# Narrow memory sums, a narrower masked copy, two more DMA transposes and a new instruction order in a planned attention and feed-forward kernel

## The chip, the cores and the metric

The kernel runs on one core of one Trainium2 chip. The metric is the device time of one execution in microseconds (us). Each engine of the core (PE for matrix products, DVE, ACT and POOL for elementwise work, SP for issuing transfers) takes its own list of instructions in the order in which the program holds them, and waits on semaphores for the others. The profile is that of one execution.

## The reference, cut to what matters

Two layers, each an attention block and a gated feed-forward block, run over 2048 tokens of width 512. Attention works on four segments of 512 tokens with 32 heads of width 16. Inside a segment it is causal softmax; across segments there is a memory: a 16x16 matrix M and a vector z for each head, to which every segment adds.

```python
for s in range(N):
    logits = jnp.einsum('bhqd,bhkd->bhqk', qs, ks) * scale + mask
    p = _softmax(logits, axis=-1)
    a_dot = jnp.einsum('bhqk,bhkd->bhqd', p, vs)
    pq = phi(qs)
    num = jnp.einsum('bhld,bhde->bhle', pq, M)
    den = jnp.einsum('bhld,bhd->bhl', pq, z)[..., None] + 1e-06
    a_mem = num / den
    o = g * a_mem + (1.0 - g) * a_dot
    outs.append(o)
    pk = phi(ks)
    M = M + jnp.einsum('bhld,bhle->bhde', pk, vs)
    z = z + jnp.einsum('bhld->bhd', pk)
...
x = x + _A_ref(_layernorm(x, axis=-1), A_wq, A_wk, A_wv, A_wo, A_beta)
x = x + _B_ref(_layernorm(x, axis=-1), B_w_gate, B_w_up, B_w_down)
```

The feed-forward block is `_gelu(x @ w_gate) * (x @ w_up) @ w_down` with an inner width of 1792. This pair of lines stands twice.

## The kernel before

All weights and all of x stay in on-chip memory. There are eight units of work k = 0..7 (two layers by four segments), each with an attention part (`Att`, L610 on) and a feed-forward part (`Ffn`, L1018 on). Everything is made of 128x128 by 128x512 products on PE.

**The planner.** The program is straight-line code whose order is made while it is built. `order` (L286) keeps a model clock for each engine (`Engine`, `Clocks`), a list of work items for PE (`Item`: due time, readiness, products, what follows) and jobs posted to the other engines. Its main loop (L1425 on) takes, at each step, two rounds of attention scores if they are due, or the ready item with the least due time, and writes its instructions out. The engines' lists come out in that order. The numbers in `POLICY` (L69) weigh these choices: due times, slacks, and margins. Three matter here. `lag` (L1446): items are first looked for that have been ready for `lag` us, then those that are ready now. `margin` (L567, L706): the transfers that make `xnT` and `vz` are taken to be there 1.4 us plus `margin` after their issue has ended; those that make `phik` and the turned memory result `amT`, 1.4 us after it. `FILL` (L65): how many tiny products stand ahead of each transposition on PE, to cover a wait. Where no item is ready and scores are still to come, a fill product of `warm` is written (L1464).

**Attention of a unit.** The rows are normalised (`Norm`), turned to the layout that PE wants (`xnT`), and multiplied by wq, wk and wv. `xnT` is made on PE by `turn_item` (four transposing products for each 128 rows, L586, then a copy out of PSUM) for the units that `by_pe` names (attention k = 1 and 2, since `pe_turns` is 2; feed-forward 0, 1 and 7), else by a transposing transfer that SP issues (`turn_later`, L431). Scores are made in 36 rounds for a unit on four row tiles (`score_round`, L938), exponentiated by ACT (L1398), masked by POOL or DVE (L1345, L1350, L1355), and summed against v by `flush_item` (L954) in four column tiles. Odd heads and the round that even and odd heads share use masked copies of k (`masked_copies`, L411 on): for even heads a copy 128 columns wide for each 128 rows, of which 64 are then overwritten by the odd heads' copy.

**Memory of a unit.** For segments 0 to 2 `phi` makes pk on ACT, POOL and DVE, SP turns it by a transfer (`phik`), and `upd_item` (L852) sums pk times v: 16 products of 128x128 by 128x128 into a PSUM bank of 4x128 columns, of which only the 16x16 blocks on the diagonal are wanted. DVE masks them with `bd` to `mblk` (L878) and keeps the running sum `macc` (L893, L895).

**PE's modes.** A product is either whole (128x128 weights, L476) or split into four 32-column tiles that run side by side (L471); `product` picks the split form when PE is in column tiles already or when a flush is near.

Of the kernel before, what the change touches and what calls it, by code (L numbers as in the profile page):

```python
# [12 lines left out]
ALU = mybir.AluOpType  # L13
# [18 lines left out]
VALUES = TPS * VW + 16  # L32
SCALE = DH ** -0.5
# [11 lines left out]
PAIRED = [(ki, P * ki, C, C * ki) for ki in range(TPS)]  # L45


def round_of(t):

    b, i = divmod(t, ROUNDS)  # L50
    if i == SHARED:
        return b, (0, 1), PAIRED, None
    par = int(i > SHARED)
    return b, (par,), FULL[i - par * (SHARED + 1)], DIAG[i - par * (SHARED + 1)]


BY_PE = {("xnTf", 0), ("xnTf", 1), ("xnTf", NK - 1)}
BANKS = 8
# [3 lines left out]
URGENT, SOON, NORMAL = -4.0, -1.5, 0.0  # L62
XN_BUFS = 4
BUFS = 6
FILL = 2  # L65
# [4 lines left out]
    flush_wait=31.348, piece_slack=5.108, kb_slack=25.115, mem_slack=-15.103, margin=2.314, qk_due=0.572,  # L70
    e_q=-1.218, e_k=1.714, exp_slack=-25.107, e_slack=9.023, phi_slack=17.383, gelu_slack=6.274,
    act_evict=8.464, first_evict=0.965, gate_step=0.061, up_due=-0.553, up_step=0.062, down_due=2.078,
# [3 lines left out]
    col_gap=3.33, hold=8, early=4.123, starve=0.308, near=-1.576, cap=4, soon=9.685, columns=0)  # L76
# [15 lines left out]
class Engine:  # L92
# [24 lines left out]
    def serve(self, now):  # L117
# [9 lines left out]
        job = min((j for j in jobs if j[0] + self.LATENCY <= start + 0.03), key=lambda j: j[0] + j[1] + (  # L127
# [123 lines left out]
class Item:  # L251


    def __init__(self, due, ready, ops, done, kind, ps, after="start"):
        self.after = after
        self.due = due if callable(due) else lambda: due
        self.ready, self.ops, self.done, self.kind, self.ps = ready, ops, done, kind, ps
        self.posted = 0.0
# [27 lines left out]
def order(pol, nc, cst, seg, wrk, psp, A_x, A_wq, A_wk, A_wv, A_wo, A_beta, B_x, B_w_gate, B_w_up, B_w_down, out):  # L286
# [88 lines left out]

    tmp_e2 = cst.tile([P, H], F32, name="tmp_e2")
    cden = cst.tile([P, H], BF16, name="cden")
    macc = cst.tile([P, 4, P], F32, name="macc")
# [32 lines left out]
    def masked_copies(ready, slack, kx, kf, told):  # L411
# [4 lines left out]
        def vector(which, eng):  # L416
            return lambda: eng.tensor_scalar(out=kx[:, :, C * which:C * which + P], in0=kf, scalar1=masks[:, which:which + 1],  # L417
                                             scalar2=None, op0=ALU.mult)
# [6 lines left out]
        ck.dve.post(ready, slack, (Port(0.35), vector(0, nc.vector), None),  # L425
                    (Port(0.35), vector(1, nc.vector), told), taken=taken)
        ck.pool.post(ready, slack + pol.kb_pool, (Port(1.57, True), vector(0, nc.gpsimd), None),
# [50 lines left out]
    def soon(name, n=KT, part=1.0):  # L478

        t = ck.pe - 0.1 - ck.back  # L480
# [20 lines left out]
    class Norm:  # L501
        def __init__(self, key, tt0, tag, slack, free):
            self.key, self.tt0, self.tag, self.slack, self.free = key, tt0, tag, slack, free
            self.mv, self.n, self.left = None, 0, TPS
# [3 lines left out]

        def stats(self, j, ready):
            def emit():  # L510
                if self.mv is None:
                    self.mv = self.small("mv", 2)
# [3 lines left out]
            def told(t):  # L516
                self.n += 1
                if self.n == TPS:
                    self.scales(t)

            ck.dve.post(ready, self.slack, (0.66, emit, None),
                        (0.17, lambda: nc.vector.bn_aggr(out=self.mv[:, j, :], in_=self.st6[:]), told))  # L522

        def scales(self, ready):
            def first():
                self.ve = wrk.tile([P, TPS, 1], F32, tag="lnve", name="ve")
                nc.gpsimd.tensor_scalar(out=self.ve[:], in0=self.mv[:, :, 1:2], scalar1=EPS_LN, scalar2=None,
                                        op0=ALU.add)

            def second():  # L530
                self.rs = self.small("rs", 1)
                nc.gpsimd.tensor_tensor(out=self.rs[:], in0=self.ve[:], in1=mhalf[:], op=ALU.pow)  # L532

            ck.pool.post(ready, URGENT, (0.25, first, None),
                         (1.05, second, lambda t: ck.when(self.free, lambda: self.start(max(t, ck.pe)))))

        def start(self, ready):
            self.xnT = seg.tile([P, KT, L], BF16, tag=self.tag, bufs=1, name="xnT")
            for j in range(TPS):
                xn_slots.take(lambda n, j=j: bufs.take(lambda i: self.row(j, n, i, max(ready, ck.pe))))  # L540

        def normed(self, j, i, eng=nc.vector):
            xn = buffer(i, "xn")
            eng.tensor_scalar(out=xn[:], in0=x_sb[:, self.tt0 + j, :], scalar1=self.mv[:, j, 0:1],  # L544
# [3 lines left out]
        def row(self, j, n, i, ready):  # L548
# [13 lines left out]
            def told(t):  # L562
                if self.by_pe():
                    items.append(self.turn_item(j, xn, t, landed))
                else:
                    turn_later(t, self.slack, lambda: self.xnT[:, :, j * P:(j + 1) * P], lambda: xn()[:], landed,
                           pol.margin)  # L567

            on_dve_or_pool(ready, self.slack, pol.xn_pool if self.key[0] == "xnTa" else None, Port(0.405),
# [5 lines left out]
        def turn_item(self, j, xn, t, landed):  # L575
# [4 lines left out]
            def turned():  # L580
# [8 lines left out]
                        lambda: evict(ps, lambda: self.xnT[:, :, j * P:(j + 1) * P], turned, landed, URGENT),  # L589
# [937 lines left out]
```

## Time and profile before

| | |
|---|---|
| time, median of 3 runs | 544.17 us (544.15 to 544.77) |
| span of the profiled execution, first to last instruction | 542.6 us |
| PE busy | 527.1 us, 97% |
| DVE busy | 443.1 us, 82% |
| ACT busy | 434.4 us, 80% |
| POOL busy | 305.9 us, 56% |

The profile lists no time for the profiled execution other than its span. The median of the runs is 1.6 us longer than that span; this is taken as what lies around the first and the last instruction. In the rows below, a group reads: line, engine, operation, output and inputs by name, shape, count, then busy time and the mean duration of one instruction. A row of the timeline begins with its start and its length in us. Products on PE overlap, so a duration is not a cost: the cost of one is the distance from its start to the next one's start.

### The profile page before, as it was taken

The page shows a single profiled execution, that of the slowest core. Times are in us where ns is not written, and L with a number is a line of the kernel's source. Part 1 is how long each engine was busy: PE and PEld are TensorE (multiplying, and loading weights), DVE is VectorE, ACT ScalarE, POOL GpSimd, SP SyncE. Part 2 cuts the span into 40 slices and gives each one's busy share as a digit, 9 for nine tenths or more (in the row PEclk, how much of TensorE's full clock was granted, in tenths as well). Part 3 has the DMA queues.
Part 4 walks back from the last instruction along what each step waited for, and adds up shares of the span by engine and source line. Part 5 has one row for each costly group of instructions (what it writes and reads, how often), then busy time and mean ns, then how long its engine had stood idle before and what let it go on. Part 6 is the DMA issues. An engine that isn't in the chain of part 4 may idle for free.

```text
span 542.6 us, 21272 instructions
## 1 busy us (share of the span) xinstructions
PE 527.1 (97%) x9271; PEld 274.9 (51%) x9332; DVE 443.1 (82%) x816; ACT 434.4 (80%) x540; POOL 305.9 (56%) x359
## 2 busy tenths in 40 slices
PE   8999989999999999999999999999999999999997
PEld 4454455454545444544544555545465456555444
DVE  7898999799988999879987998889586797786342
ACT  6999989988998989989799798996879977930320
POOL 4897786369846788349993468716753265300000
PEclk9999999999999999999999999999999999999999
DMA  8306510610331123310312250211420105100001
GB/s 268 98 13 192 117 23 17 171 35 20 51 50 24 24 40 61 41 38 9 41 32 50 33 71 4 40 33 23 79 52 3 22 13 89 24 3 25 16 0 40
DMA packets 64784, 26.94 MB, mean 50 GB/s; under 512 B 49074, under 2 KB 64690, under 8 KB 64690
## 3 DMA queue, kind: packets, MB, share of 16 engines
q1 hardware_dynamic: 64400, 25.31, 22.7%
q8 instruction: 73, 1.20, 0.9%
q10 hardware_dynamic: 290, 0.26, 0.2%
q14 instruction: 21, 0.17, 0.1%
HBM read 9.70 MB, written 2.10 MB: 22 GB/s over the span
## 4 chain that ended last, share of the span: by engine, by line
PE 83%; DVE 12%; issue 2%; DMA 2%; ACT 0%; POOL 0%; SPq 0%; DVEq 0%; ACTq 0%
PE ps L476 44%; PE ps L471 25%; PE ps L938 7%; PE ps L954 6%; DVE st L514 2%; DVE x_sb L1027 1%; DVE xn L544 1%; DVE byq L971 1%; DMA phik<-e 1%; DVE phiq L745 1%; DVE mv L522 1%; DMA x_sb<-in_A_x_dram 0%; DMA amT<-am 0%; DVE e L745 0%; ACT pt L1398 0%
## 5 line engine op out<-in xcount | busy, mean ns | idle before, releaser
L1398 ACT ACTIVATE pt<-ps 128x1024 bf16<-128x1024 f32 x288 | 279.1, 1026 | 44.3 <-PE ps L938 40.3
L1345 POOL TENSOR_SCALAR_AFFINE_SELECT pt<-pt 128x256 bf16<-128x256 bf16 (+1 forms) x192 | 108.6, 579 | 117.1 <-ACT pt L1398 110.4
L1092 DVE TENSOR_TENSOR gel_sb<-gel_sb,ps 128x512 bf16<-128x512 bf16 x112 | 75.2, 681 | 34.0 <-PE ps L476 25.0
L476 PE MATMUL ps<-xnT,wu_sb 128*128 128x512 bf16 x287 | 66.8, 379 | 1.4 <-issue 1.1
L476 PE MATMUL ps<-xnT,wg_sb 128*128 128x512 bf16 x261 | 62.6, 379 | 1.3 <-issue 0.5
L764 POOL TENSOR_SCALAR e<-e 128x512 bf16<-128x512 bf16 x37 | 57.6, 1557 | 1.6 <-ACT e L741 0.6
L971 DVE STREAM_TRANSPOSE byq<-ps 128x512 f32<-128x512 f32 x64 | 45.0, 706 | 16.3 <-PE ps L954 15.6
L476 PE MATMUL ps<-wd_sb,gel_sb 128*128 128x512 bf16 (+1 forms) x293 | 56.8, 340 | 1.3 <-issue 1.0
L1027 DVE TENSOR_TENSOR x_sb<-x_sb,ps 128x512 bf16<-128x512 bf16 (+1 forms) x68 | 42.8, 640 | 16.5 <-PE ps L476 14.8
L1350 POOL TENSOR_SCALAR_AFFINE_SELECT pt<-pt 64x1024 bf16<-64x1024 bf16 x40 | 47.7, 1194 | 15.1 <-ACT pt L1398 13.8
L471 PE MATMUL ps<-wd_sb,gel_sb 128*32 128x512 bf16 (+1 forms) x792 | 47.1, 378 | 0.6 <-issue 0.6
L476 PEld LDWEIGHTS <-wu_sb 128*128 128x128 bf16 x301 | 28.3, 98 | 33.8 <-issue 0.7
L471 PE MATMUL ps<-xnT,wg_sb 128*32 128x512 bf16 x700 | 42.4, 380 | 0.1
L514 DVE BATCH_NORM_STATS2 st<-x_sb 128x6 f32<-128x512 bf16 x60 | 40.4, 673 | 0.1
L476 PEld LDWEIGHTS <-wg_sb 128*128 128x128 bf16 x273 | 25.3, 98 | 29.1 <-DVE byq L971 0.6
L476 PEld LDWEIGHTS <-gel_sb 128*128 128x128 bf16 x306 | 28.3, 98 | 22.6 <-issue 1.1
L954 PE MATMUL ps<-pt,vaug 128*32 128x256 bf16 (+2 forms) x1344 | 34.8, 238 | 0.3 <-POOL pt L1345 0.3
L471 PE MATMUL ps<-xnT,wu_sb 128*32 128x512 bf16 x588 | 34.1, 379 | 0.0
L417 POOL TENSOR_SCALAR kx<-kf,masks 128x512 bf16<-128x512 bf16 x20 | 33.0, 1649 | 1.2
L1151 ACT ACTIVATE gel_sb<-gel_sb 128x2048 bf16<-128x2048 bf16 (+1 forms) x21 | 33.2, 1643 | 0.0
L954 PEld LDWEIGHTS <-vaug 128*32 128x32 bf16 x1344 | 27.9, 97 | 10.5 <-issue 2.3
L544 DVE TENSOR_SCALAR xn<-x_sb,mv,rs 128x512 bf16<-128x512 bf16 x58 | 31.4, 592 | 2.2 <-POOL rs L532 1.9
(149 smaller groups left out, 877.0 us busy)
## 6 DMA issues: line engine op xcount, KB each, us to landing
vz<-vaug SPq DMA_DIRECT2D x14, 136.0 KB, 2.7
wg_sb<-in_B_w_gate_dram SPq DMA_DIRECT2D x8, 224.0 KB, 4.0
wu_sb<-in_B_w_up_dram SPq DMA_DIRECT2D x8, 224.0 KB, 5.0
wd_sb<-in_B_w_down_dram SPq DMA_DIRECT2D x7, 256.0 KB, 4.7
x_sb<-in_A_x_dram SPq DMA_DIRECT2D x3, 512.0 KB, 6.6
out_dram<-x_sb SPq DMA_DIRECT2D x12, 128.0 KB, 1.9
xnT<-xn SPq DMA_TRANSPOSE x40, 2.5
wk_sb<-in_A_wk_dram SPq DMA_DIRECT2D x2, 256.0 KB, 5.1
```

Source lines behind the costliest of these rows:

```text
L471: nc.tensor.matmul(out[r], lhsT=lhsT[:, r], rhs=rhs, start=start, stop=stop, tile_position=(0, 32 * c))
L476: nc.tensor.matmul(out, lhsT=lhsT, rhs=rhs, start=start, stop=stop)
L514: nc.vector.bn_stats(out=self.st6[:, 0, :], in_=x_sb[:, self.tt0 + j, :])
L764: lambda eng: eng.tensor_scalar(out=e[0][:], in0=e[0][:], scalar1=1.0, scalar2=None, op0=ALU.min), summed)
L938: nc.tensor.matmul(ps_all[:, bank, o + c0:o + c0 + n], lhsT=lhsT, rhs=self.q[rows, b, q0:q0 + n], start=True, stop=True, tile_position=(32 ...
L954: nc.tensor.matmul(ps()[32 * j:32 * j + 32, q0:q0 + n], lhsT=va[:, ki * VW + g:ki * VW + g + 32], rhs=pt_all[:, places[i], j, c0:c0 + n], ...
L971: nc.vector.transpose(out=self.byq[:, par, :, :].rearrange("p a c -> p (a c)"), in_=ps()[:])
L1027: ck.dve.post(ck.made(), slack, (0.15 + 0.00104 * (c1 - c0), lambda: nc.vector.tensor_tensor(out=xt, in0=xt, in1=ps()[:, 0:c1 - c0], op=AL ...
L1092: ck.dve.post(ck.made(), NORMAL, (0.683, lambda: nc.vector.tensor_tensor(out=g, in0=g, in1=ps()[:], op=ALU.mult), lambda t: (ps.read(t), e ...
L1345: nc.gpsimd.affine_select(out=view, in_=view, pattern=[[0, 4], [0, n], [1, C]], compare_op=ALU.is_ge, fill=0.0, base=C, channel_multiplier=-1)
L1350: nc.gpsimd.affine_select(out=view, in_=view, pattern=[[0, 4 * TPS], [1, C]], compare_op=ALU.is_ge, fill=0.0, base=0, channel_multiplier=-1)
L1398: nc.scalar.activation(out=pt_all[:, s0:s0 + 2, 2 * p:2 * p + 2, :].rearrange("p r h c -> p h r c"), in_=ps_all[:, pair[0]:pair[1] + 1, :] ...
```

## The change

**Memory sums.** Each of the 16 steps becomes four products of 128x32 by 128x32, one for each column tile, which keep only the pairs of heads on the diagonal. The PSUM result and `macc` shrink from 512 to 128 columns, and one DVE instruction spreads `macc` over `mblk`.

```diff
-            def m(c):
-                j, b = divmod(c, 4)
-                product(blocks()[:, b, :], self.phik[:, j, b * P:(b + 1) * P],
-                        by_head(self.vaug)[:, j, 4 * b:4 * b + 4, :, 0:DH], c == 0, c == n_mm - 1)
+            def m(j, b):
+                ck.tiling("columns")
+                for c in range(4):
+                    nc.tensor.matmul(pairs()[32 * c:32 * c + 32, b, :], lhsT=self.phik[:, j, b * P + 32 * c:b * P + 32 * c + 32],
+                                     rhs=by_head(self.vaug)[:, j, 4 * b + c, :, 0:DH], start=(j == b == 0),
+                                     stop=(j == TPS - 1 and b == 3), tile_position=(0, 32 * c))
+                ck.count += 4
...
+                def spread():
+                    nc.vector.tensor_tensor(out=made[0][:].rearrange("p b (c d) -> p b c d", d=32),
+                                            in0=macc[:].unsqueeze(2).to_broadcast([P, 4, 4, 32]),
+                                            in1=bd[:].rearrange("p (c d) -> p c d", d=32).unsqueeze(1).to_broadcast([P, 4, 4, 32]),
+                                            op=ALU.mult)
```

**Masked copies.** On DVE and POOL the even heads' copy is written 64 columns wide, as ACT did already.

```diff
         def vector(which, eng):
-            return lambda: eng.tensor_scalar(out=kx[:, :, C * which:C * which + P], in0=kf, scalar1=masks[:, which:which + 1],
-                                             scalar2=None, op0=ALU.mult)
+            n = P if which else C
+            return lambda: eng.tensor_scalar(out=kx[:, :, C * which:C * which + n], in0=kf[:, :, 0:n],
+                                             scalar1=masks[:, which:which + 1], scalar2=None, op0=ALU.mult)
```

**Order.** All numbers of `POLICY` are new, `FILL` goes from 2 to 0, and `pe_turns=0` hands the transposition of the attention inputs 1 and 2 to SP's transfers. A few of the numbers:

```diff
-FILL = 2
+FILL = 0
...
-    flush_wait=31.348, piece_slack=5.108, kb_slack=25.115, mem_slack=-15.103, margin=2.314, qk_due=0.572,
...
-    down_step=0.526, upd_due=0.786, kb_act=6.552, vz_slack=-10.454, x_dve=-0.565, v0_due=-1.4, x1_at=-45.234,
-    x2_at=18.289, x3_at=24.819, x3_load=-3.83, direct=4, gelu_tiles=4, look=1.769, lag=0.5, wv_at=8.591,
-    xn_pool=7.037, kb_pool=5.303, cut_pool=1.107, at_pool=10.661, pe_turns=2, gate_due=0.765, shun=0.534,
...
+    flush_wait=137.725, piece_slack=-52.409, kb_slack=33.295, mem_slack=-22.008, margin=-0.607, qk_due=1.219,
...
+    upd_due=16.162, kb_act=27.141, vz_slack=2.192, x_dve=-0.406, v0_due=-4.209, x1_at=-117.128, x2_at=19.103,
+    x3_at=0.157, x3_load=-132.211, direct=2, gelu_tiles=2, look=0.514, lag=-0.432, wv_at=-9.865, xn_pool=5.659,
+    kb_pool=37.59, cut_pool=-0.436, at_pool=14.287, pe_turns=0, gate_due=0.761, shun=17.251, col_gap=5.787, hold=14,
```

**Readiness.** Output products (`wo`) of a half of the rows may start when that half of the attention output is there (without halved units both halves come at once), and the gates of feed-forward 0 from the sixth weight tile on need no longer wait for the first memory sum (the first ones write over v's columns).

```diff
-                return Item(k + 0.61 + 0.001 * j, lambda: soon(("aT", k)),
+                return Item(k + 0.61 + 0.001 * j, lambda: soon(("aTh", k, j // 2), eager=k in HALVED),
...
-                            lambda: ck.has(("xnTf", k)) and (("down", k - 1) if k else ("upd", 0)) in ev,
+                            lambda: ck.has(("xnTf", k)) and (k == 0 and ft >= HELD or (("down", k - 1) if k else ("upd", 0)) in ev),
```

**Tables.** Rounds and flushes are read from tables (`whole_block`, `table`) in place of `round_of`. The tables can split a unit's queries into halves and use a quicker normalisation for units named in `HALVED`; `HALVED` is empty, so that rounds and flushes have the shapes they had. Two small constants (`junk`, `means`) that only the quicker normalisation reads are set up.

More of the change, by code (lines that the diff above doesn't have):

```diff
@@ L528, in first @@
                                         op0=ALU.add)
             def second():
[L531 to L539, printed above, removed]
+                if self.rs is None:
+                    self.rs = self.small("rs", 1)
@@ new lines, in second, with start @@
+                nc.gpsimd.tensor_tensor(out=self.rs[:, j0:j0 + n, :], in0=self.ve[:], in1=mhalf[:, 0:n, :], op=ALU.pow)
+            ck.pool.post(ready, min(self.urge(j0), URGENT), (0.25, first, None),
+                         (0.45 + 0.15 * n, second, lambda t: ck.when(self.free, lambda: self.start(max(t, ck.pe), j0, n))))
+        def start(self, ready, j0, n):
+            if self.xnT is None:
+                self.xnT = seg.tile([P, KT, L], BF16, tag=self.tag, bufs=1, name="xnT")
+            for j in range(j0, j0 + n):
@@ L944, in flush_item @@
             ps = Psum()
-            number = 8 * k + 2 * b + par
+            places = self.places
+            half = L // 2
+            c0, c1 = (0, L) if h is None else (half * h, half * h + half)
+            na = (c1 - c0) // 32
+            work = []
+            for par in pars:
+                for t in used:
+                    for b2, par2, ki, q0, nq, o in TABLES[k][0][t][0]:
+                        if b2 == b and par in par2 and c0 <= q0 < c1:
+                            work.append((par, t, vz if len(par2) > 1 else self.vaug, ki, q0 - c0 + (par * half if h is not None else 0),
+                                         nq, o))
@@ L956, in mm @@
                                          stop=(m == len(work) - 1), tile_position=(0, 32 * j))
[L958 removed]
+            slack = CHAIN if last and k in HALVED else SOON
             def done():
[L961 to L962 removed]
+                for t in used:
+                    slot = places[t]
                     slot_users[slot] -= 1
@@ L1447, in order @@
                 got = [it for it in items if it.after in ev and it.ready() and (
-                    it.kind != "flush" or not streams or tight() or it.posted < late or ck.mode == "columns")]
+                    it.kind != "flush" or it.chain or not streams or tight() or it.posted < late or ck.mode == "columns")]
                 if got:
```

293 lines of the change are left out of this document (186 added, 107 removed).

## The prediction

> **What bounds the kernel now.** I read the head of the page first: who is busy, and where in the span.
>
> ```profile
> span 542.6 us, 21272 instructions
> PE 527.1 (97%) x9271; PEld 274.9 (51%) x9332; DVE 443.1 (82%) x816; ACT 434.4 (80%) x540; POOL 305.9 (56%) x359
> PE   8999989999999999999999999999999999999997
> PEclk9999999999999999999999999999999999999999
> ```
>
> PE is busy almost everywhere and its clock is never throttled. Next the span cut where the digits dip.
>
> ```profile
> 69.00:81.00 12.00, 9.99 (x259) 6.71 (x261) 11.79 (x27) 10.72 (x14) 10.00 (x13) 1.00 0.07 12
> 132.00:140.00 8.00, 6.67 (x193) 4.28 (x192) 7.81 (x17) 7.11 (x10) 5.56 (x10) 1.00 0.02 4
> 140.00:480.00 340.00, 335.00 (x6438) 174.46 (x6477) 286.67 (x505) 299.73 (x358) 203.53 (x235) 1.00 0.23 38
> ```
>
> The columns are length, then busy time of PE, weight loads, DVE, ACT and POOL. From 140 to 480 us PE misses 5.0 us of 340, and most of that is no wait: 39 of 6477 weight loads have no product beside them, records that are missing. PE waits in two short places, 69 to 81 (2.0 us) and 132 to 140 (1.3 us), where feed-forward 0 and 1 begin; there DVE has no time left. So the time is PE's list of products. What shortens that list shortens the run; what relieves other engines counts at those two places alone.
>
> The price of one product is the distance from start to start. I read it off the timeline where one kind follows another.
>
> ```profile
> 508.19 1.89 PE L476 MATMUL ps<-xnT,wu_sb 128*128 128x512 bf16 x8
> 509.91 1.89 PE L476 MATMUL ps<-xnT,wg_sb 128*128 128x512 bf16 x8
> 216.59 4.07 PE L471 MATMUL ps<-xnT,wg_sb 128*32 128x512 bf16 x72
> 220.49 0.62 PE L954 MATMUL ps<-pt,vaug 128*32 128x256 bf16 x24
> 212.25 0.61 PE L476 MATMUL ps<-mblk,phiq 128*128 128x128 bf16 x8
> 212.70 1.46 PE L476 MATMUL ps<-xnT,wg_sb 128*128 128x512 bf16 x6
> 214.09 0.40 PE L938 MATMUL ps<-q,kx 32*128 32x64 bf16 x12
> 395.11 1.19 PE L471 MATMUL ps<-vaug,phik 128*32 128x128 bf16 x64
> 396.07 0.65 PE L471 MATMUL ps<-wd_sb,gel_sb 128*32 128x512 bf16 x7
> 376.51 0.29 PE L954 MATMUL ps<-pt,vz 128*32 128x64 bf16 x16
> 376.62 1.69 PE L471 MATMUL ps<-wd_sb,gel_sb 128*32 128x512 bf16 x28
> 372.86 0.68 PE L471 MATMUL ps<-zcols,phiq 128*32 128x8 bf16 x64
> 373.45 1.05 PE L471 MATMUL ps<-xnT,wq_sb 128*32 128x512 bf16 x16
> ```
>
> A whole product of 512 columns costs (509.91 - 508.19) / 8 = 0.215 us; four column tiles of 512 together cost (220.49 - 216.59) / 18 = 0.217. The two forms are equal, so a shift between them is free. A whole one of 128 columns costs 0.45 / 8 = 0.056; four tiles of 128 cost 0.96 / 16 = 0.060, of 64 0.11 / 4 = 0.028, of 8 0.59 / 16 = 0.037. A change of mode costs 214.09 - 212.70 - 6 x 0.215 = 0.10.
>
> **The change part by part.** Counts are those of the two programs' lists.
>
> Memory sums: six units (three segments, two layers) of 16 steps are 96 steps, before 65 whole and 31 split. They cost 65 x 0.056 + 31 x 0.060 = 5.5 us. Afterwards all 96 are four tiles of 32 columns. That size is not in the trace; its neighbours are 64 columns (0.028) and 8 columns (0.037), both with a fresh weight load for each tile. From below 0.014, a quarter of 0.056, from above 0.060, no gain: 1.3 to 5.8 us. I take 0.033, between the neighbours: 3.2 us, **-2.3** (range -4.2 to +0.3).
>
> [...]
>
> Transposes and fillers: 48 PE transposes remain of 80, and all 24 tiny products ahead of them go.
>
> ```profile
> L586 PE MATMUL ps<-ident,xn 128*128 128x128 bf16 x80 | 6.3, 219 | 0.8 <-DVE xn L544 0.5 <-DVE byq L971 0.3
> L584 PE MATMUL ps<-warm 128*128 128x32 bf16 x24 | 2.5, 179 | 0.2 <-ACT pt L1398 0.2
> 137.81 0.22 PE L476 MATMUL ps<-warm 128*128 128x128 bf16 x1
> 137.96 0.44 PE L938 MATMUL ps<-q,kf 16*128 16x64 bf16 x8
> ```
>
> 32 transposes at 0.056 (128 columns, as above; 6.3 / 80 = 0.079 is the most) are **-1.8** (-1.8 to -2.5). The fillers' 2.5 us hold waits that stay, since the three feed-forward units that PE turns are the same. Two of them mostly stand for about 0.05 us ahead of four transposes; I take 24 x 0.025 = **-0.6** (0 to -2.5).
>
> Changes of mode rise from 302 to 315: 13 x 0.10 = **+1.3**. Fill products, which the planner writes where it has nothing ready, rise from 31 to 33. Each costs its 0.056 and what PE still waits, at most 0.215: **+0.3** (0 to +0.4). The rest of PE's products are the same in number and columns.
>
> Waits. At 69 to 81 twelve fill products go, where the lists reach the first gate 3.4 us of PE work earlier; but around feed-forward 1 nine more stand, and five more elsewhere. One wait there is DVE's copy of the memory sum:
>
> ```profile
> 77.16 0.27 PE L938 MATMUL ps<-q,kf 16*128 16x64 bf16 x5 [0.45 <-DVE macc L893]
> L893 DVE COPY macc<-ps 128x512 f32<-128x512 f32 x2 | 1.3, 666 | 0.0
> 135.97 0.40 PE L586 MATMUL ps<-ident,xn 128*128 128x128 bf16 x4 [0.54 <-DVE xn L544]
> ```
>
> The copy becomes a quarter as wide, so that this 0.45 us shrinks; the wait for xn at 135.97 stays, as that turn stays on PE. I take **-0.4** in all (+2 to -3: all of the 3.3 us at the two places could go, and as much could come).
>
> Off PE: 14 more PSUM copies on DVE at 0.68 (in each of seven units two more gates are copied out instead of going straight through ACT) are 9.5 us on an engine that has 53 us free from 140 to 480. Masked copies of 64 columns halve a POOL instruction of 1.65 us, 13 times. POOL is 56% busy and its tiles are read rounds later. Both are hidden by PE's list and **cost nothing**; if that cover went, DVE's 9.5 us would show.
>
> ```profile
> L461 DVE CAST gel_sb<-ps 128x512 bf16<-128x512 f32 x39 | 26.5, 682 | 7.4 <-PE ps L471 4.2 <-PE ps L476 2.5
> L417 POOL TENSOR_SCALAR kx<-kf,masks 128x512 bf16<-128x512 bf16 x20 | 33.0, 1649 | 1.2
> ```
>
> SP: eight more transposing transfers, ahead of and between the first vz and weight pieces.
>
> ```profile
> 17.72 1.40 DVE L544 TENSOR_SCALAR xn<-x_sb,mv,rs 128x512 bf16<-128x512 bf16 x3
> 18.84 1.35 SPq L701 DMA_DIRECT2D vz<-gel_sb  x2
> 38.25 5.22 SPq L437 DMA_TRANSPOSE xnT<-xn  x4
> 23.84 1.04 PE L471 MATMUL ps<-xnT,wq_sb 128*32 128x512 bf16 x16
> 25.14 0.29 PE L954 MATMUL ps<-pt,vz 128*32 128x64 bf16 x16
> xnT<-xn SPq DMA_TRANSPOSE x40, 2.5
> vz<-vaug SPq DMA_DIRECT2D x14, 136.0 KB, 2.7
> ```
>
> Four issues take 5.22 us, and a row lands 2.5 us after its issue begins. If the first row of input 1 is ready near 18.1, as before, the last is issued at 22.0 and lands at 24.5. The new list has the first product that needs all four rows after as much PE work as the old one, 23.8 us: a wait of 0 to 0.7. vz, now issued at 23.3 in place of 18.84, lands near 26.7 (its second half, issued 0.7 later); its first reader stands 0.7 us of PE work later than it did, at 25.9. I take **+0.5** for both (0 to 1.5). The weight pieces behind them are not read before the gates of feed-forward 0, after 69 us.
>
> Sum: -2.3 - 1.8 - 0.6 + 1.3 + 0.3 - 0.4 + 0.5 = -3.0 us, a span of 539.6; with the 1.6 us by which the median exceeds the profiled span, **541.2 us**.
>
> **The rivals.**
>
> *Late transfers (slower).* The new margins take xnT and vz to be there 2.1 us after an issue begins (1.3 + 1.4 - 0.6; before 5.0), and items may be opened 0.43 us ahead of readiness (before 0.5 behind). Measured landing is 2.5 to 2.7. A reader opened at once would wait 0.4 + 0.43 = 0.8 us and more, and PE would stand with everything queued behind it: scores, so ACT. Five feed-forward turns, seven attention turns, eight vz and 64 flushes after masks could be hit. Beyond 4 us of it the gain is gone; if half of the 20 transfers lost 0.8 us and a third of the flushes 0.15, it is 8 + 3 = 11 us less 3: 552; with a half of that, 546.7. Against it:
>
> ```profile
> 196.89 5.14 SPq L437 DMA_TRANSPOSE xnT<-xn  x4
> 206.46 1.26 PE L471 MATMUL ps<-xnT,wg_sb 128*32 128x512 bf16 x20
> 258.96 6.36 SPq L437 DMA_TRANSPOSE xnT<-xn  x4
> 272.76 1.46 PE L476 MATMUL ps<-xnT,wg_sb 128*128 128x512 bf16 x6
> ```
>
> The last of four issues begins some 1.2 us before the group ends and lands 2.5 us after it began: at 203.3 and 266.6. Gates begin 3.2 and 6.2 us later. The plan may move by 2.92 (margin) and 0.93 (lag), 3.85 us: the second case has room, the first would wait 0.7.
>
> *The start eats the gain.* Inputs 1 and 2 both come late, vz too, ACT runs dry for 2 to 3 us: 543.2 to 544.2.
>
> [...]
>
> *The plan closes its gaps.* Of the 3.3 us at the two places 2.5 go: 538.5. For it: the earlier first gate. Against: nine more fill products at feed-forward 1.
>
> *Nothing but order.* The halved tables and the quick normalisation are switched off; if the sums too gave nothing (0.060), 543.7.
>
> **How the numbers follow.** Forecast 0.55 (540 to 542.8); gaps closed 0.16; start, or sums that give nothing, 0.15; late transfers 0.12; floor 0.02. A measurement of this kernel can tell 0.2%, 1.1 us: faster means under 543.1. The first two cases and 0.03 of the third give faster 0.74; same is 0.11 of the third; slower 0.15 are its last 0.01 and the last two. The range goes from 537.0 (gaps closed with sums at the low bound) to 545.0, which leaves out most of the late transfers. The likeliest case's own range is 540 to 542.8.
>
> **What would show it.** [...] PE's time from 140 to 480 should lack as little as before; waits for xnT, vz or masks of 0.2 us and more there mean late transfers. Input 1's first four-row product should come at 23.8 to 24.6 us. DVE at 450 us must not show in waits of PE. I am wrong if PE's idle time grows by more than 3 us.

## The result, and the profile after

| | before | after |
|---|---|---|
| time, median | 544.16 us (4 runs, 543.93 to 544.77) | 551.62 us (4 runs, 549.07 to 553.53) |
| ratio, 95% interval | | 1.013 (1.0114 to 1.0147) |
| span of the profiled execution | 542.6 us | 547.3 us (its time: 549.07 us) |

Slower, by 1.3%: outside the range, and on the other side of the forecast. First the page's head, then the three windows that the prediction read.

```profile
span 547.3 us, 21708 instructions
PE 522.4 (95%) x9450; PEld 268.2 (49%) x9518; DVE 447.4 (82%) x844; ACT 427.5 (78%) x528; POOL 300.6 (55%) x357
PE   8989999997899999999999998999999999999997
PEclk9999999999799999999999999999999999999999
```

```profile
69.00:81.00 12.00, 10.92 (x291) 6.32 (x291) 10.97 (x24) 11.06 (x16) 8.30 (x11) 1.00 0.12 25
132.00:140.00 8.00, 3.79 (x90) 2.43 (x92) 5.39 (x13) 5.84 (x7) 7.53 (x10) 0.73 0.40 51
140.00:480.00 340.00, 331.08 (x6576) 171.35 (x6622) 291.48 (x528) 289.29 (x344) 196.05 (x229) 1.00 0.22 37
```

PE's busy time fell (527.1 to 522.4 us), and yet the span is 4.7 us longer: by the heads of the two pages PE's idle time went from 15.5 to 24.9 us. Part of that is not real: 68 of the 9,518 products have no record in this profile, and 40 gaps of 0.16 us, 6.3 us in all, stand where records are missing; before has 27 such gaps, 4.3 us. Without them the idle time grew by some 7 us. And the clock row, all 9 before, has one slice of 7, from 137 us on. The table of PE's waits (place, releaser, us in total, times, longest) says for what PE stood; before, no single wait was above 1.1 us.

```profile
PE ps L527 <- DMA xnT<-xn: 3.0, 1, 3.0
PE ps L527 <- DVE e L840: 2.1, 1, 2.1
PE ps L522 <- issue: 1.8, 2, 1.3
```

Three kinds of stand, then, which the timeline places. **First, unit 2's first q product**: PE's rows of that time (PEld is PE's loading of weights), and SP's.

```profile
38.43 0.28 PE L527 MATMUL ps<-warm 128*128 128x128 bf16 x2
40.83 0.82 PE L527 MATMUL ps<-xnT,wq_sb 128*128 128x512 bf16 x3 [2.13 <-DVE e L840]
...
40.83 0.33 PEld L527 LDWEIGHTS <-wq_sb 128*128 128x128 bf16 x3 [2.30 <-DMA xnT<-xn]
...
36.51 1.20 SPq L488 DMA_TRANSPOSE xnT<-xn  x1
37.75 2.30 SPq L351 DMA_DIRECT2D wg_sb<-in_B_w_gate_dram  x2
```

The releaser named for the product, DVE's `e`, ended at the same moment. The weight load ahead of the product names the transfer, and so does the product itself at this place in three of the runs below. It is the fourth turned row of input 2, issued at 36.51 and landed near 40.8, after 4.3 us and not 2.5. The two pieces of wg behind it took 2.30 us to issue, where two pieces of wo, at 33.46 us, took 1.04. **Second, the v product of unit 4's second 128 rows**, and the clock behind it (windows: length, busy of PE, weight loads, DVE, ACT, POOL, then the granted clock).

```profile
135.52 0.48 PE L527 MATMUL ps<-warm 128*128 128x128 bf16 x4 [0.31 <-DVE byq L1080]
139.02 1.49 PE L527 MATMUL ps<-wv_sb,xnT 128*128 128x512 bf16 x3 [3.01 <-DMA xnT<-xn]
...
134.55 6.58 SPq L488 DMA_TRANSPOSE xnT<-xn  x4
```

```profile
135.70:139.00 3.30, 0.30 (x4) 0.17 (x3) 1.60 (x4) 2.14 (x3) 3.22 (x6) 0.50 0.76 80
139.00:142.60 3.60, 3.58 (x72) 2.29 (x72) 1.90 (x4) 0.00 (x0) 0.69 (x2) 0.51 0.36 75
142.60:146.00 3.40, 3.35 (x53) 1.80 (x53) 3.30 (x8) 3.25 (x5) 1.16 (x3) 1.00 0.00 0
```

Four issues take 6.58 us here; 5.22 us is what four take undisturbed (the prediction's row of before). PE stands 3.0 us, and then works 3.6 us at half its clock, which loses another 1.8. Behind the shorter stand at 38 us the clock stayed at 1.00. The length of one stand does not decide it: the clock is at 0.50 from 135.7 us on, before the long stand begins, and in the 3.4 us ahead of that, a stretch half as long as the 6.8 us for which it is halved, PE was busy for 2.2. In the runs below it is halved behind stands of 1.7 and of 1.0 us as well. **Third, a stand for nothing that the profile shows**, right behind the narrow sums.

```profile
331.06 0.67 PE L961 MATMUL ps<-vaug,phik 128*32 128x32 bf16 x64
331.55 0.36 PE L522 MATMUL ps<-mblk,phiq 128*32 128x128 bf16 x12
333.21 0.24 PE L522 MATMUL ps<-mblk,phiq 128*32 128x128 bf16 x4 [1.30 <-issue]
```

The group of sums starts at 331.06 and the next one at 331.55: 16 steps in 0.49 us, 0.031 us each, the price that the prediction took (0.033). Then PE stops in the middle of a group of equal products, 12 done and 4 to come, for 1.3 us. Another such stand of 0.5 us ends at 198.3 us.

The account: the list was forecast 3.1 us shorter (all terms but waits and start). 4.7 + 3.1 = 7.8 us came in. The rows have 2.1 + 3.0 + 1.8 + 1.3 + 0.5 = 8.7, less one stand of 0.6 us that before had, shown below: 8.1. This is an estimate, since the 3.1 us are themselves a forecast.

### The profile page after: what moved, and what is told of

The parts are those of the page before. It is cut to its first block, busy times and chain, and to the rows that moved or that the text cites. A ratio compares the mean times of both kernels' runs of the same rounds, so it can differ in the third digit from the quotient of the medians.

```text
span 547.3 us, 21708 instructions
## 1 busy us (share of the span) xinstructions
PE 522.4 (95%) x9450; PEld 268.2 (49%) x9518; DVE 447.4 (82%) x844; ACT 427.5 (78%) x528; POOL 300.6 (55%) x357
## 3 DMA queue, kind: packets, MB, share of 16 engines
q8 instruction: 74, 1.21, 1.0%
## 4 chain that ended last, share of the span: by engine, by line
PE 79%; DVE 8%; issue 4%; ACT 4%; DMA 3%; POOL 1%; SPq 0%; DVEq 0%; ACTq 0%; POOLq 0%
PE ps L527 41%; PE ps L522 23%; PE ps L1032 7%; PE ps L1061 6%; ACT pt L1527 1%; DMA phik<-e 1%; DVE x_sb L1152 1%; DMA xnT<-xn 1%; DVE st L588 1%; DVE gel_sb L512 1%; DVE byq L1080 1%; DVE phiq L840 1%; ACT gel_sb L1282 1%; PE ps L961 1%; POOL pt L1476 1%
## 5 line engine op out<-in xcount | busy, mean ns | idle before, releaser
L527 PE MATMUL ps<-xnT,wg_sb 128*128 128x512 bf16 x299 | 72.7, 380 | 1.8 <-issue 1.4
L1152 DVE TENSOR_TENSOR x_sb<-x_sb,ps 128x512 bf16<-128x512 bf16 (+1 forms) x68 | 43.2, 645 | 24.9 <-PE ps L527 16.2
L527 PE MATMUL ps<-xnT,wu_sb 128*128 128x512 bf16 x252 | 58.7, 379 | 1.2 <-issue 0.8
L1481 POOL TENSOR_SCALAR_AFFINE_SELECT pt<-pt 64x1024 bf16<-64x1024 bf16 x36 | 42.6, 1182 | 10.1 <-ACT pt L1527 8.0
L527 PEld LDWEIGHTS <-wg_sb 128*128 128x128 bf16 x317 | 28.4, 98 | 32.7 <-issue 1.3
L522 PE MATMUL ps<-xnT,wu_sb 128*32 128x512 bf16 x732 | 41.8, 379 | 0.0
L1282 ACT ACTIVATE gel_sb<-gel_sb 128x1024 bf16<-128x1024 bf16 (+1 forms) x43 | 40.9, 1034 | 0.0
L512 DVE CAST gel_sb<-ps 128x512 bf16<-128x512 f32 x53 | 35.3, 680 | 5.1 <-PE ps L527 4.1
L527 PEld LDWEIGHTS <-wu_sb 128*128 128x128 bf16 x265 | 24.8, 98 | 29.9 <-issue 1.1
L1032 PE MATMUL ps<-q,kx 32*128 32x64 bf16 (+2 forms) x1120 | 31.0, 218 | 1.1 <-DVE x_sb L1152 0.5
L522 PE MATMUL ps<-xnT,wg_sb 128*32 128x512 bf16 x524 | 31.8, 379 | 0.0
```

The costliest lines, as they stand in the source:

```text
L522: nc.tensor.matmul(out[r], lhsT=lhsT[:, r], rhs=rhs, start=start, stop=stop, tile_position=(0, 32 * c))
L527: nc.tensor.matmul(out, lhsT=lhsT, rhs=rhs, start=start, stop=stop)
L1032: nc.tensor.matmul(ps_all[:, bank, o + c0:o + c0 + n], lhsT=lhsT, rhs=self.q[rows, b, q0:q0 + n], start=True, stop=True, tile_position=(32 ...
L1152: ck.dve.post(ck.made(), slack, (0.15 + 0.00104 * (c1 - c0), lambda: nc.vector.tensor_tensor(out=xt, in0=xt, in1=ps()[:, 0:c1 - c0], op=AL ...
L1282: return (0.205 + 0.427 * (f1 - f0), lambda: nc.scalar.activation(out=g, in_=g, func=ACT.Gelu_apprx_tanh), lambda t: self.gelu_done(t, f0, ...
```

## The experiments

Two theories at the start. *Late transfers*: the new numbers put readers right behind the landing that the plan assumes. *The code itself loses*: narrow sums or more transfers cost more than their rows say. "The yardstick" below is the changed kernel run beside the first experiments; the later ones ran on other chips, on which before took the same 544.2 to 544.3 us.

### The changed kernel again

> The changed kernel unaltered, as the yardstick for the runs beside it. Late-transfer theory: the two long waits come back in every run, at unit 2's first q product (38.5 us, 2.1 to 2.3 us) and at unit 4's second v product (135.7 us, 3.0 us), because both readers stand where a transposing transfer needs all of its usual 2.5 us and more; time 549 to 553.5, as in the four runs shown. Chance theory (one unlucky execution was profiled): the waits at the two places differ by more than 1 us from those of the profile, and the time falls under 548 in some runs.

550.41 us (6 runs, 548.62 to 552.44); before on the same chip 544.25 (11 runs, 543.69 to 544.66). The long waits came back, 1.5 us at unit 2 and 3.0 us at unit 4, and so did the stands without a reason: 0.65 us up to 198.3, 0.83 up to 332.6, and one more, 0.65, up to 463.5. This profile has a record of every product, and PE is idle for 16.0 us of 546.9. Not chance, though the size varies: the changed kernel spreads over 3.8 us, before over 1.

### Sums as wide as they were

```diff
-                    nc.tensor.matmul(pairs()[32 * c:32 * c + 32, b, :], ...
-                                     rhs=by_head(self.vaug)[:, j, 4 * b + c, :, 0:DH], ...
+                    n = min(4, 16 - 4 * b - c)
+                    nc.tensor.matmul(psm()[32 * c:32 * c + 32, P * b:P * b + 32 * n], ...
+                                     rhs=by_head(self.vaug)[:, j, 4 * b + c:4 * b + c + n, :, 0:DH], ...
```

> Order unaltered; the memory sums alone are widened again: four column tiles of 128 columns (fewer at the last three tiles, where the values end) in place of 32, of which the same 32 are used. If the narrow sums are worth what their rows say (0.031 to 0.033 us a step against 0.060), 96 steps cost 2.6 to 2.8 us more, and the time is the yardstick's plus 2 to 3 us. If PE's 64 short products in 0.5 us drain its instructions and cause the stand of 1.3 to 1.5 us right behind the sums at 331 us (and the 0.5 us at 197 us), that stand shrinks or goes, and the sum of both is +0.5 to +1.5. If narrow sums are worth nothing, no change within 0.5.

550.83 us (549.64 to 551.08): +0.4, where the rows promise 2.6 to 2.8. The same products in this run:

```profile
332.22 1.04 PE L962 MATMUL ps<-vaug,phik 128*32 128x128 bf16 x61
...
334.06 0.24 PE L522 MATMUL ps<-mblk,phiq 128*32 128x128 bf16 x4 [0.53 <-issue]
```

The slower sums take 0.4 us longer, and the stand behind them is 0.3 us shorter than the yardstick's 0.83 at exactly the same product; the one at 463 is gone. That fits the theory that part of what narrow sums save is spent waiting behind them. It is no proof: the same stand was 1.30 us in the first profile of the changed kernel, so 0.3 us between two profiles is within what it varies by.

What PE waits for there can be counted. The trace has 74 packets, 1.21 MB, on the queue that is taken to carry PE's instructions:

```profile
q8 instruction: 74, 1.21, 1.0%
```

16.4 KB each; PE's list has 9,518 products and as many weight loads, so a packet would hold 257 of them. Between the start of one packet and that of the next, 255 of PE's instructions begin on the mean and 256 in the median. In the trace's records of single packets, all seven of these stands (two in the changed kernel, three in its repetition, two here) begin 228 to 231 instructions after such a fetch began, and end 2.4 to 3.2 us after it. By these counts, an estimate, PE has in this order some 230 instructions in hand when the fetch of the next block begins. A block lasts 7.4 us on the mean (547 us / 74), but these 230 were used up in 1.7 us from 330.0 us on, where products of four tiles follow each other: four instructions and four loads for each. PE then stood 1.3 us. The number 230 belongs to this order: in the kernels further below, and in before, such stands of 0.25 us and more begin 0 to 209 instructions after the fetch began, and 422 to 533 after the one before it. They too end 2.2 to 3.5 us after the begin of a fetch.

### Products that keep the clock up

```diff
+                    if (k, j) == (4, 1):
...
+                            for _ in range(12):
+                                nc.tensor.matmul(ps()[:], lhsT=warm[:], rhs=wide, start=True, stop=True)
```

> Order unaltered; twelve products of 512 columns on constants (12 x 0.215 = 2.6 us) are added ahead of the v product of unit 4 that waits 3.0 us at 135.7 us. Their result is overwritten. Clock theory: the wait itself cannot be shortened by them, but PE's granted clock, 0.50 from 135.7 to 142.6 us, stays at 1.00, so that the 3.6 us of work behind the wait run at full speed: the yardstick less 1.5 to 2 us. If the halved clock costs nothing (other engines set the pace there): no change, or +0.3 where a run waits less than 2.6 us.

546.73 us (545.91 to 547.18), 3.7 less: more than the clock alone.

```profile
137.82 2.75 PE L812 MATMUL ps<-warm 128*128 128x512 bf16 x12
140.85 1.04 PE L527 MATMUL ps<-wv_sb,xnT 128*128 128x512 bf16 x4 [0.28 <-DMA xnT<-xn]
```

```profile
140.80:144.00 3.20, 3.06 (x78) 2.12 (x79) 2.46 (x5) 0.61 (x1) 1.04 (x2) 1.00 0.40 86
```

The clock behind unit 4 stays at 1.00. In this run it is halved elsewhere instead, for 3.4 us from 41.2 us on, behind a stand of 1.7 us at unit 2. A further gain: the stands at 198, 331 and 463 us are gone. Nothing was done to these places, except that all instructions behind 138 us stand 24 further on in the list.

### The old margin for one group

```diff
-                           pol.margin)
+                           2.314 if self.key == ("xnTa", 4) else pol.margin)
```

> The old margin of 2.314 is put back for one transfer group alone, the turned rows of attention unit 4; all lists are as in the changed kernel up to 135 us and made anew behind it (9 fill products more stand in PE's list). Late-transfer theory: the wait at 135.7 us (3.0 us) and the halved clock behind it (1.7 us) go; the 9 fill products take back up to 9 x 0.22 = 2 us: the yardstick less 2.5 to 5 us, 546 to 549. Rival (DVE has no time left from 128 to 140 us, PE would stand there whatever it waits for): the wait moves to another product within 3 us and the time is the yardstick's within 1 us.

552.12 us (551.0 to 552.89), no gain. At 135.7 us the wait is gone (the longest there is 0.5 us). But the order behind it is a new one, and it has its own late reader, at a feed-forward unit:

```profile
460.51 0.23 PE L522 MATMUL ps<-warm 128*32 128x128 bf16 x4
463.75 1.86 PE L522 MATMUL ps<-xnT,wg_sb 128*32 128x512 bf16 x13 [3.01 <-DMA xnT<-xn]
...
458.83 3.61 SPq L488 DMA_TRANSPOSE xnT<-xn  x2
```

```profile
463.70:468.00 4.30, 4.25 (x52) 1.94 (x56) 1.38 (x2) 0.00 (x0) 0.00 (x0) 0.62 0.45 115
```

3.0 us, and a clock of 0.62 behind it. Neither theory as written: the wait did not move to a neighbour, and mending one group mends nothing, since the margin holds for all. A fetch of instructions began at 460.1, in the middle of these two issues (3.61 us; by the undisturbed four it would be 2.6).

### Where the blocks begin

At this point the suspicion was a third theory: the fetch disturbs the transposing transfers too. Over all transposing issues of the traces of before and after: with no fetch under way from 1.4 us ahead of the issue to its end, 0 of 45 (before) and 1 of 46 (after) took over 1.6 us; with one, 12 of 43 and 14 of 50. The landings of the rows of `xnT` say it more plainly. In the trace of before, the 23 rows in whose first 2.4 us no fetch was under way landed 2.44 us after their issue began in the median, 2.49 at most; the 13 with one, 3.18 and 4.93. In the trace of the changed kernel it is 2.36 and 3.35 for 23 rows without, 3.81 and 4.42 for 21 with. Over all thirteen traces, 203 of 275 rows with a fetch and 11 of 279 without took over 3.2 us.

To move the fetches and nothing else:

```diff
-    keep_warm(WARM, 0)
+    keep_warm(WARM - 10, 0)
+    for _ in range(8 * 10):
+        nc.tensor.matmul(ps_all[:, 0, 0:64], lhsT=warm[:], rhs=wide[:, 0, 0:64], start=True, stop=True)
```

> Order unaltered, but ten of the twelve warming products at the very start are each cut into eight of 64 columns: 70 products and 70 weight loads more before the first real one, in the time that PE waits for its inputs anyway. PE's list is fetched in blocks of 16 KB, 256 of its instructions; all later blocks begin 140 instructions earlier in the work. Fetch theory: the stands of PE without a reason (0.8 to 1.5 us at 197.3, 331.5 and 462.7 us, each 228 to 231 instructions after a fetch began) go, 2.1 to 2.7 us in all, though up to 1.4 us may appear near 395 to 404 us; and as no fetch then begins between 36.4 and 40 us, the wait for unit 2's fourth row shrinks from 1.7 to 2.3 us to 0.5 to 1. The wait at unit 4 stays, as a fetch still begins within 1 us of the row's issue. Time: the yardstick (550.4) less 1.5 to 4 us. Rival (the stands belong to the instructions, or to the transfers, and not to the block borders): the same stands at the same products, time within 1 us of the yardstick.

547.65 us (547.29 to 548.36): 2.8 less than the yardstick, by nothing but the places of the block borders. All three stands without a reason are gone; the place of 331 us now reads:

```profile
331.12 0.67 PE L963 MATMUL ps<-vaug,phik 128*32 128x32 bf16 x64
331.62 0.42 PE L524 MATMUL ps<-mblk,phiq 128*32 128x128 bf16 x16
331.84 0.40 PE L524 MATMUL ps<-wd_sb,gel_sb 128*32 128x512 bf16 x4
```

A smaller one is new (about 0.3 us at 407). The waits for turned rows followed the fetches as well:

```profile
135.30 5.29 SPq L490 DMA_TRANSPOSE xnT<-xn  x4
137.65 1.89 PE L529 MATMUL ps<-wv_sb,xnT 128*128 128x512 bf16 x4 [1.00 <-DMA xnT<-xn]
...
17.18 6.50 SPq L490 DMA_TRANSPOSE xnT<-xn  x4
24.21 1.05 PE L524 MATMUL ps<-wv_sb,xnT 128*32 128x512 bf16 x16 [1.17 <-DMA xnT<-xn]
25.74 0.62 PE L524 MATMUL ps<-xnT,wq_sb 128*32 128x512 bf16 x8 [0.48 <-DMA xnT<-xn]
```

At unit 4 the four issues take 5.29 us (6.58 in the changed kernel), the row that PE needs lands 2.3 us after its issue began (4.0), and PE waits 1.0 instead of 3.0, against the expectation that this wait would stay. At unit 2, as expected, the wait shrinks: 0.45 us and, at the first q product, 0.35 instead of 1.5 to 2.1. In exchange a fetch now begins at 21.0 us, the rows of input 1 are slow (6.50 for 5.22), and PE waits there 1.7 us, where the changed kernel waited for nothing. What is left at unit 4, 1.0 us, and at unit 2's q product, 0.35, has no fetch beside it: that much the plan itself is late. The clock is halved behind unit 4 here too, for 3.4 us instead of 6.8:

```profile
137.60:141.00 3.40, 3.35 (x60) 2.09 (x60) 2.27 (x4) 0.99 (x2) 2.84 (x5) 0.50 0.66 104
```

### Shift and cover together

> The shift of the block borders and the twelve covering products ahead of unit 4's late v product together; order otherwise unaltered. If the two losses are separate they add: the covered kernel (546.7) less 0.5 to 2 us, since that kernel showed few stands for instructions already: 544.5 to 546. If what the cover gained beyond the clock's 1.7 us was its own shift by 24 instructions, nothing more is left: 546 to 547.

547.23 us (545.11 to 548.09): no better than either alone, and the two losses do not add as the first case expected. The cover does keep the clock up: it is 1.00 behind unit 4, where the shifted kernel had 0.50 for 3.4 us, a loss of 1.7. But its twelve products take 2.75 us, and with the shift only 1.0 us of waiting is left for them to fill. By these rows, an estimate, they cost as much as they save.

### Wide sums where no stand is left

The two edits above together.

> The shifted kernel (140 instructions more at the start; 547.65) with the sums widened to 128 columns as in the first wide run; order unaltered. There hardly a stand for instructions is left that a slower sum could fill. If the narrow sums are worth what their rows say, this costs the full 2.6 to 2.8 us: 550 to 550.7. If they are worth nothing: 547.3 to 548.

549.82 us (549.15 to 551.73) against 547.65: 2.2 us in the medians and 1.9 between the quickest runs, most of the 2.6 to 2.8 and just short of the range expected. Where the instructions came in time, the narrow sums were worth most of what their rows say.

### Old code, new numbers

> The code of before with the changed kernel's POLICY and FILL (no narrow sums, wide masked copies; margin -0.607, lag -0.432, inputs 1 and 2 turned by SP). Late-transfer theory (the numbers make the waits, whatever the code): waits of PE of 1.5 us and more for xnT or vz, as in the changed kernel, one at unit 2's q and at least one later; with PE's list about as long as before's but 16 fill products more (47 against 31, up to 0.22 us each) and wide sums: 549 to 556. Rival (the new code makes the loss): no wait over 1.2 us, time within 2 us of before, 542 to 546.

555.45 us (554.17 to 558.92), the slowest of all. The time is in the range of the late-transfer theory, but its waits are only in part: 2.0 us for `xnT` at unit 2's q, and the others for DVE and ACT.

```profile
PE ps L586 <- DVE xn L544: 3.7, 3, 1.9
PE ps L938 <- ACT pt L1398: 2.2, 4, 1.1
PE ps L471 <- DMA xnT<-xn: 2.0, 1, 2.0
```

The numbers do harm without the new code; but as a set of numbers fits the code for which it was found, this tells little of why.

### New code, margins near those of before, other numbers fitted anew

This kernel keeps all of the new code and of the hand-over to SP (`pe_turns=0`), sets `margin=2.0`, `lag=0.4` (before: 2.314 and 0.5) and `FILL=2`, and has the other numbers fitted anew to these.

> The changed code with margin 2.0 and lag 0.4 (those of before were 2.314 and 0.5, those of the change -0.607 and -0.432), FILL 2, and the other numbers of POLICY fitted anew to these. SP still turns inputs 1 and 2, the sums are narrow. PE's list is as long as the changed kernel's: 300 changes of mode against 314, 35 fill products against 33, by the prices of the prediction 3.9 us shorter than before's. Late-transfer theory (the code is sound, the loss is in readers put too close behind their transfers): no wait of PE over 1.2 us behind 10 us, clock 1.00 throughout, 540 to 543. Rival (the new code itself loses: more instructions to fetch, more transposing transfers): waits for instructions and transfers of 3 us and more in all come back at other places, 545 to 550.

542.94 us (11 runs, 542.15 to 544.21), ratio to before 0.9979 (0.9971 to 0.9988): faster than both kernels, if little. The page's head, PE's waits and the windows:

```profile
span 540.8 us, 22271 instructions
```

```profile
PE ps L680 <- DVE xn L638: 1.4, 2, 0.9
PE ps L1032 <- issue: 0.8, 1, 0.8
```

```profile
132.00:140.00 8.00, 6.95 (x148) 4.35 (x142) 7.73 (x16) 7.84 (x11) 6.71 (x11) 1.00 0.02 4
140.00:480.00 340.00, 334.22 (x6871) 173.65 (x6910) 282.99 (x510) 298.61 (x356) 192.73 (x229) 1.00 0.20 38
```

No wait for `xnT` at all, and the clock at 1.00. Its transfers are no quicker. The tile's view of unit 4's rows, issue and landing (least, median, most), first here, then before:

```profile
L488 SPq DMA_TRANSPOSE xnT<-xn x4: 1200/1227/2296, 141.0 to 144.9; - x4
DMA to landing us min/median/max: 2.3/3.7/6.0
```

```profile
L437 SPq DMA_TRANSPOSE xnT<-xn x4: 1217/1228/1235, 140.6 to 144.6; - x4
DMA to landing us min/median/max: 2.4/2.5/4.9
L471 PE MATMUL ps<-xnT,wq_sb x12: 379/379/379, 175.4 to 175.9; 128*32 128x512 bf16 x12
```

One took 6.0 us, with a fetch of instructions beside it, and no reader noticed: in both kernels they are read some 26 to 31 us after the last issue (from 170.8 us on here). So the new code is not what loses. As all the other numbers changed with the margins, it is not shown that the margins alone would do.

### Controls: the shift on kernels with room

> Control: the kernel before with the same start as the shifted kernel (ten warming products cut into eight each, 140 instructions more), order unaltered. If the cut products cost nothing by themselves and before has slack behind its transfers, as its waits say (none over 1.1 us), the time stays within 0.8 us of before's 544.2; its one stand without a reason (0.8 us at 396.3 us, behind the only sum that it makes in 64 four-tile products) may go: 543.4 to 545. If the shift had gained its 2.8 us by something other than the borders (a warmer PE, an earlier start), before would gain as much: 541 to 542.

543.65 us (543.16 to 544.32), ratio 0.999 (0.9981 to 0.9999): 0.7 us, no more. Its one stand goes; before, then shifted:

```profile
397.34 1.04 PE L471 MATMUL ps<-wd_sb,gel_sb 128*32 128x512 bf16 x13 [0.62 <-issue]
```

```profile
395.04 1.19 PE L473 MATMUL ps<-vaug,phik 128*32 128x128 bf16 x64
396.01 1.30 PE L473 MATMUL ps<-wd_sb,gel_sb 128*32 128x512 bf16 x20
```

So the cut warming products gain nothing by themselves, and this kernel, whose readers have room, hardly depends on the borders.

> The refitted kernel (542.94) with 70 instructions more at the start (five warming products cut into eight), order unaltered. Its trace shows two stands for instructions, 0.8 us at 401.9 and 0.4 us at 170.1. Fetch theory: both go or move, and no more than 1 us can be had or lost, since no reader stands close behind its transfer: 541.9 to 543.9. Against it: a change of more than 1.5 us either way, which would mean that this order too hangs on where its blocks begin.

544.18 us (12 runs, 543.49 to 546.83): 1.2 us worse, just outside the range, and three of the twelve took 546.7 to 546.8. This profile is of one of those three. Of the two stands one went and one moved (0.6 us, up to 406.0), three of 0.2 to 0.6 are new, and so is a long one where five groups of four-tile products follow each other:

```profile
314.76 0.40 PE L524 MATMUL ps<-wd_sb,gel_sb 128*32 128x512 bf16 x3 [2.12 <-issue]
```

Here the fetch itself came late: 510 instructions after the one before, where 255 are the mean in the changed kernel's trace, so that PE stood 0.3 us after it had begun. The granted clock of this execution is 0.994 in the mean, and 1.000 in the one of 543.49 us. The refitted order is free of late readers, not of the fetch.

## Why the prediction was wrong

**Which step failed.** "Waits. I take -0.4 in all (+2 to -3)", and with it the 0.12 for the late transfers. The mechanism of that rival, readers too close behind their transfers, is a good part of what happened, and its range of 546.7 to 552 holds the 551.6. That the range fits is luck: it was made of ten transfers at 0.8 us and some twenty flushes at 0.15, and what came was two waits of 2.1 and 3.0 us, the clock, and the stands for instructions. I argued it away with "a row lands 2.5 us after its issue begins". That is a median: the tile's view of before has 4.9 us as its longest (2.49 is the longest with no fetch of instructions beside it), and I did not ask what would become of a reader that has no room when one of these comes. And "against it" I set two feed-forward groups with 3.2 and 6.2 us of room; the readers that stood are those of attention units 2 and 4. Unit 4 had 30 us of room in before, which the new numbers took away in full. A margin that is too small for the longest landing doesn't cost a share of each transfer's lateness, as my 0.8 us a transfer had it. Here it cost little at most of them, and 2.1 and 3.0 us where a transfer met a fetch, plus the clock. Of the 2.1 us at unit 2 and the 3.0 at unit 4, the shift left 0.35 (and 0.45 at a product ahead of it) and 1.0, with no fetch beside the rows.

**What the prediction didn't have.** That PE can stand for its instructions: 1.8 us in the profile of the changed kernel, 2.1 in that of its repetition, and by way of the turned rows more. The shift shows it. That the clock can be halved around such a stand: 1.8 us. The cover shows that products in the stand prevent it there.

**The list of products.** The sums at 0.033 us a step measured 0.031, and narrow against wide tiles 2.2 us (547.65 against 549.82), of 2.6 to 2.8 by the rows, where hardly a stand is left behind them. In the changed kernel's own order it was 0.4, which fits a shorter sum that buys a longer stand. The floor, which has 0.02 among the chances, is a term that no run shows; in its place the same row shows 0.031 us for the four narrow products of a step together. The other terms were not measured one by one. The whole list can be estimated from PE's busy time with the gaps of missing records added: 527.1 + 4.3 = 531.4 us before; 522.4 + 6.3 = 528.7 after, of which 1.8 is the halved clock, so 4.5 us shorter; in the repetition 530.9, of which some 2 is the halved clock, so 2.5 shorter. The 3.1 that was forecast lies between. The refitted kernel, whose list is 3.9 us shorter than before's by the same prices, has a span of 540.8 us, where the sum was 539.6.

**DVE's and POOL's work costs nothing**: right; the table of waits has no entry for DVE's fourteen more evictions, and PE misses 0.5 of 20 us from 440 to 460 us. **The start**: input 1's first four-row product came at 23.72 us, with no wait, just ahead of the 23.8 to 24.6 that was named; the 0.5 us taken for it was not lost there but, four times as large, one input later, at unit 2. **The gaps at feed-forward 0 and 1** did not close: PE misses 1.1 us of 12 instead of 2.0 in the first, and 4.2 of 8 instead of 1.3 in the second. The rival that the plan closes its gaps is refuted.

"I am wrong if PE's idle time grows by more than 3 us": it grew by 9.4 on the pages, some 7 without the missing records.

Two of its side sums do not come out: the rival of the closed gaps is 541.2 - 2.5 + 0.4 = 539.1, not 538.5, since 0.4 of waits is in the sum already; and two more fill products at up to 0.056 + 0.215 each are 0.5 at most, not 0.4. Neither bears on the result.

**What stays open.** Why a fetch slows a transposing issue was not tried, only that it does. What decides whether the clock is halved is open too: a stand of 2.1 us at unit 2 left it alone, one of 1.7 us there did not. The profiled execution is the quickest of the four. The slower ones lost up to 4.5 us more; their mean granted clock is 0.991 instead of 0.994, which would be one more stretch of 3.4 us at half clock, 1.7 us, and the rest no trace shows. That the changed kernel spreads over some 4 us fits collisions that fall differently each time, and is only argued; the shifted one spreads over 1.1, but with the cover over 3.0.

## What to carry to other kernels

Before trusting that a transfer stays hidden, take its longest landing in the profile of before (here 4.9 us), not the median (2.5), and ask of each reader how much room the new order leaves it: a planner's margin is bought for the worst transfer, and cutting it gains nothing on the others. Count instructions, not only columns: splitting a product in four makes eight instructions of two, and in the changed kernel a stretch that used up 230 of them in 1.7 us ended in a stand of 1.3 us for the next block. When a time changes with nothing but the number of instructions ahead of a place, shift the list by half a block before explaining it otherwise.

## What the runs showed of the hardware

- PE's instructions come in packets of 16.4 KB (74 packets, 1.21 MB in the changed kernel), 255 instructions from one to the next on the mean. In the changed kernel PE stood 228 to 231 instructions after a fetch began, until 2.4 to 3.2 us after its begin, though the packet itself took only 0.9 to 1.7 us. In the other kernels the count was 0 to 209, and the end 2.2 to 3.5 us.
- Of the transposing issues that met such a fetch, 12 of 43 (before) and 14 of 50 (changed kernel) took 1.6 to 2.4 us instead of 1.2; of those without a fetch near, 0 of 45 and 1 of 46 took over 1.6. A row with a fetch in its first 2.4 us landed after 3.81 us in the median in the changed kernel, one without after 2.36. The two rows that PE stood for, each with a fetch beside it, landed 4.0 and 4.3 us after their issue began.
- The clock was halved for 3.4 us or twice that, 13 times in the thirteen traces, their first 10 us and their ends left out. In the 3.4 us ahead of each, PE was busy for 15 to 68% of the time; of the other stretches of that length, nine with 48 to 67% were followed by no halving.
